# A causal attention with two feed-forward layers on one core: token blocks of 512 and 256 at 256-byte addresses, GpSimd subtractions in shorter passes, and eight PSUM banks in turn

## The chip, the core and the metric

The kernel runs on one core of a Trainium2 chip. Its engines have queues of their own and meet only at semaphores: TensorE (PE in the rows, its weight loads PEld), VectorE (DVE), ScalarE (ACT), GpSimd (POOL) and SyncE (SP), which here only issues DMA transfers. The metric is the time of one execution on the device in microseconds (us).

## The reference

```python
def _attn_ref(q, k, v, f):                       # 4 batches, 8 heads, 576 tokens, head size 64
    scores = (1.0 / np.sqrt(D)) * np.matmul(q, k.transpose(0, 1, 3, 2))
    cum = np.cumsum(np.log(np.clip(f, 0.0001, 1.0)), axis=-1)
    decay = cum[:, :, :, None] - cum[:, :, None, :]
    scores = np.where(causal, -1000000000.0, scores + decay)   # causal: above the diagonal
    attn = np.exp(scores - np.max(scores, axis=-1, keepdims=True))
    attn = attn / (np.sum(attn, axis=-1, keepdims=True) + 1e-09)
    return np.matmul(attn, v)
def _moe_ref(x, w_in, w_out):                    # x: 2304 x 512, d_ff 2048
    h = x @ w_in
    return (h * (1.0 / (1.0 + np.exp(-h)))) @ w_out
def _moe2_ref(x, w_a, w_b, w_out):               # d_ff 1536
    return ((x @ w_a) * (x @ w_b)) @ w_out
```

The attention's output, all heads side by side, is the x of the first layer, and its output the x of the second.

## The kernel before

Numbers that need more than one TensorE pass are held as a high part (rounded to the float32r format) and a low part (the rest). A product of two such numbers is three matmuls: high by high, low by high, high by low (`mm3`, lines 310 to 312; `mms`, lines 754 to 756).

**Attention.** 16 pairs of heads pass one after the other. For each pair, `load_parts` fetches q and k (`qk`, 1216 columns), makes the high part `qkh` (line 508, on ScalarE or VectorE) and the low part `qkl` (line 509, one GpSimd subtraction of all 1216 columns). `score` multiplies them into PSUM tiles `s` in groups of query blocks: 64x512, 64x384, 64x256 and 64x128 columns for the two heads of a pair side by side, and 128x288 for the last, shared block. Each is four steps: the decay in bf16, and three products of the parts. VectorE takes the masked maxima (line 584), ScalarE the exponentials (line 592). `transpose` (tiles `t_x`, `t_y`) and `attend` (tile `pv`) follow; VectorE multiplies by the inverse sums into `xf` (line 687), ScalarE makes the high part of x (line 690), GpSimd the low part (line 692, 576 columns at once).

**First chunk and decoding.** The weights come as 64-bit words and are decoded into high and low parts, 256 columns at a time: a transfer (`d`, lines 268 and 705), ScalarE (272, 707), VectorE (273 to 278, 709 to 716), ScalarE's cast (279, 718), GpSimd (280 and 281, 719 and 720). Chunk 0 of the feed-forward weights (two f-tiles of 128) is decoded and used inside the attention: `first_chunk` works on blocks of 288 tokens, four `ps` groups of three matmuls for each of two f-tiles, then g by ScalarE (766), VectorE (768), the cast `ghi` (770) and `glo` (772), then `po`, two groups for each of four output tiles. The first four of the eight blocks have a PSUM bank of their own; the last four take banks from a cycle (`BANKS`): the tag `s` has four banks, `t` two, `pv` and `mm` one each. The chunks after it are decoded into tiles `d0` to `d3`, two of each, once the attention's tiles are given up (`plan_late`).

**Order.** Up to the end of the first chunk a planner (`Plan`) sets the order on each engine from priorities and estimated times, and `keep_warm` puts idle matmuls into its first gaps. Each engine works through its row in order: an instruction that waits holds up all behind it.

**Feed-forward.** `model_kernel` then loops over chunks 1 to 12 and, in each, over the token blocks of `BLOCKS`: for each f-tile of a chunk `ff_in` (12 matmuls per product, tile `ps`, the moving operand is `x[:, part, kc, t0:t0+n]`), then `ff_out` of the block before (tile `po`, the moving operand is `ghi` or `glo`). That is 760 groups of three in `ps` and 520 in `po`, 3840 matmuls in all, 768 for each of the five blocks.

**Addresses.** `warm` is one float (4 bytes of a partition), and the tile allocator rounds up to 32 bytes. In the built program all that is allocated behind it (`x`, `acc`, the weights from chunk 1 on, `ghi`, `glo`, `g`) begins 32 bytes past a multiple of 64; `x` and the weights 32 bytes past a multiple of 256. Blocks of 464 tokens begin at 0, 1856, 3712, 5568 and 7424 bytes of a row of x, that is at 0, 64, 128, 192 and 0 bytes past a multiple of 256, counted from x's own start.

Of the kernel before, what the change touches and what calls it, by code (L numbers as in the profile page):

```python
# [9 lines left out]
F32 = mybir.dt.float32  # L10
# [3 lines left out]
AF = mybir.ActivationFunctionType  # L14
# [13 lines left out]
Q2, QK = 512 + S, 512 + S + P  # L28
# [3 lines left out]
PARTS = ((0, 128), (128, 448))  # L32
# [7 lines left out]


TAIL = NT // 2
BLOCKS = [(t, min(464, NT - t)) for t in range(0, NT, 464)]

# [159 lines left out]
def t_dve(n, fast=False):  # L206
    return 65 + n / (1.92 if fast else 0.96)
# [6 lines left out]
def t_pool(n):  # L214
    return 133 + 2.135 * n
# [14 lines left out]
def model_kernel(ctx: ExitStack, tc: tile.TileContext, qk, q0, v, f, w, out):  # L230
    nc = tc.nc
    chunks, _ = chunk_layout()

    const = ctx.enter_context(tc.tile_pool(name="const", bufs=1))
# [9 lines left out]
    dec = dram.tile([NH, 6, 2, S], BF16, name="dec")  # L244

    invs = dram.tile([NH // 2, 9, P], F32, name="invs")
    warm = const.tile([NH, 1], F32, name="warm")
    temp = ExitStack()
    dp = temp.enter_context(tc.tile_pool(name="dp", bufs=1))
    ft, one, cum = (dp.tile([NH, S], F32, name=n) for n in ("ft", "one", "cum"))  # L250
# [65 lines left out]
    gp = [None, 0, 0]  # L316
# [61 lines left out]
    NB = 288  # L378
# [12 lines left out]
    plan = Plan()  # L391
# [12 lines left out]
    def prepare():  # L404

        pr = -9
# [15 lines left out]
        plan.add("DVE", 369, lambda: nc.vector.tensor_scalar(ft, ft, 1e-4, 1.0, ALU.max, ALU.min), (), ["f"], pr)  # L422
        plan.add("ACT", 1900, lambda: nc.scalar.activation(ft, ft, AF.Ln), (), ["f"], pr)

        plan.add("ACT", 1400, lambda: nc.scalar.activation(warm, one[:, 0:1], AF.Exp), ["one", "f"], ["warm"], pr)
        plan.add("DVE", 669, lambda: nc.vector.tensor_tensor_scan(cum, one, ft, 0.0, ALU.mult, ALU.add), ["f", "one"], ["cum"], pr)
        plan.add("POOL", 133, lambda: nc.gpsimd.tensor_copy(warm, cum[:, 0:1]), ["cum"], ["warm", "go"], pr)
        plan.add("DVE", 400, lambda: nc.vector.memset(maskw, 0.0), ["cum"], [("const", 3)], -7)
        plan.add("DVE", 250, lambda: nc.vector.memset(mask2, 0.0), ["cum"], [("const", 3)], -7)
        plan.add("POOL", 250, lambda: nc.gpsimd.tensor_copy(maskw[:, -P:], maskb), [("const", 0), "cum"], [("const", 3)], -7)  # L430
# [64 lines left out]
    def load_parts(pair, pr):  # L495

        raw = buf(sb, "qkr", [P, QK], F32, f"qk_{pair}")
        hi, lo = (buf(sb, n, [P, QK], F32R, f"{n}_{pair}") for n in ("qkh", "qkl"))
        n = len(tags["dt"].bufs) % SLOTS["dt"]
        dt = Buf(tags["dt"], lambda: decays[n])  # L500
        heads[2 * pair] = heads[2 * pair + 1] = dict(s1=hi, raw=raw, hi=hi, lo=lo, dt=dt)
        plan.dma(480, 4 * P * QK, lambda: nc.sync.dma_start(raw(), qk[pair]), ["go" if pair == 1 else "dec"], [raw], pr)
        for p in range(2):
            plan.dma(400, 0, lambda p=p: nc.sync.dma_start(
                dt()[p * D:p * D + 6, :2 * S], dec[2 * pair + p].rearrange("r i t -> r (i t)")), ["dec", ("decay", n)], [(dt, p)], pr)
            plan.dma(400, 0, lambda p=p: nc.sync.dma_start(
                dt()[p * D:p * D + 6, 2 * S + p * D:2 * S + (p + 1) * D], dec[2 * pair + p, :, 0, 512:]), ["dec", ("decay", n)], [(dt, 2 + p)], pr)
        plan.add("ACT", t_act(QK, 93), lambda: nc.scalar.copy(hi(), raw()), [raw], [(hi, "h")], pr, also=[("DVE", t_dve(QK, True), lambda: nc.vector.tensor_copy(hi(), raw()))])
        (e1, d1, f1), two = ((e, d, lambda eng=eng: eng.tensor_sub(lo(), raw(), hi().bitcast(F32)))
                             for e, d, eng in (("POOL", t_pool(QK), nc.gpsimd), ("DVE", t_dve(QK) + 100, nc.vector)))  # L510
        plan.add(e1, d1, f1, [(hi, "h"), raw], [(lo, "l")], pr)

    def score(pair, group):

# [8 lines left out]
        for ib in group:  # L523
# [16 lines left out]
            for p, part, step in todo:  # L540
# [21 lines left out]
                if whole:  # L562
                    keys += [(t["s1"], "dec", 0), (t["s1"], "dec", 1), (t["s1"], "h")]
                else:
                    keys += [(t["dt"], n) for n in range(4)] + [(t["hi"], "h"), (t["lo"], "l")]
            keys = list(dict.fromkeys(keys))
            dur = 2 * (nj / 0.6 + 20) if whole else 8 * t_mm(nj) if shared else 4 * t_mm(nj)
            plan.add("PE", dur, lambda mms=mms: [mm() for mm in mms], keys, banks, pr + PRIO["s"],
# [74 lines left out]
    def attend(pair):  # L643
# [42 lines left out]
        for ps, (h0, hn) in zip(out, PARTS[::-1]):  # L686
# [2 lines left out]
                [ps] + [(rb, p, i) for p in range(2) for i in range(2)], [(xf, h0)], pr + PRIO["fin"])  # L689
        plan.add("ACT", t_act(S, 93), lambda: nc.scalar.copy(xp(0), xf()),  # L690
                 [(xf, h0) for h0, _ in PARTS], [("x", 0, b, kc)], pr + PRIO["fin"])
        plan.add("POOL", t_pool(S), lambda: nc.gpsimd.tensor_sub(xp(1), xf(), xp(0).bitcast(F32)),
                 [(xf, h0) for h0, _ in PARTS] + [("x", 0, b, kc)], [("x", 1, b, kc)], pr + PRIO["fin"])

    W0, W1, PER = 256, 256, 3

# [45 lines left out]
    def wkeys(col):  # L742
        return [("w0", col // W0), ("w0", col // W0, 1)]

    def first_chunk(b, t0, bank, sub):
# [12 lines left out]
        for t in range(nf):  # L758
            ps = bank(f"ps_{t}_{tok}")
            g = buf(gA, "g", [P, NB], F32, f"g_{t}_{tok}")  # L760
            for kc in range(KC):
                plan.add("PE", 3 * t_mm(NB), lambda ps=ps, t=t, kc=kc: mms(
                    ps, w_first(0, 0, t, kc), lambda: (big["x"][:, 0, kc, tok:tok + NB], big["x"][:, 1, kc, tok:tok + NB]),
                    kc == 0, kc == KC - 1),
                    [("x", i, b, kc) for i in range(2)] + wkeys(kc * nf * P + t * P), [ps], pr)
            plan.add("ACT", t_act(NB), lambda ps=ps, g=g: nc.scalar.activation(g(), ps()[:, :NB], AF.Tanh, scale=0.5),
                     [ps], [g], pr)
            plan.add("DVE", t_dve(NB), lambda ps=ps, g=g: nc.vector.scalar_tensor_tensor(
# [30 lines left out]
    fill_decays()  # L799

    FILL = 4
    BANKS = ('s', 't')
    fill = [(b, t0) for b in range(B) for t0 in range(0, S, NB)]
    GROUPS = (4,), (3,), (2,), (1, 0)
    for pair in range(NH // 2):
# [40 lines left out]


    mmpool[0] = ctx.enter_context(tc.tile_pool(name="mmB", bufs=8, space=PSUM))
    gp[:] = ctx.enter_context(tc.tile_pool(name="gB", bufs=2)), 3, 464
    prev = []  # L850
    for c in range(1, len(chunks)):
        pend = []
# [57 lines left out]
```

## Time and profile before

| | |
|---|---|
| median of 3 runs | 1052.15 us (1051.17 to 1052.24) |
| profiled execution, own time | 1050.7 us |
| its span, first to last instruction | 1049.0 us |
| mean granted TensorE clock | 0.996 |
| TensorE busy | 1034.1 us (99%), 5814 matmuls |
| VectorE, ScalarE, GpSimd busy | 650.6, 438.6, 325.9 us |

The own time is the span and 1.7 us around it. TensorE is hardly ever idle, so its time is the kernel's, but a matmul's record is longer than its turn: the records overlap. What a matmul costs in a dense stretch is the stretch divided by its matmuls.

### The profile page before, as it was taken

How to read it: one execution, taken by the hardware profiler on the slowest of the kernel's cores; microseconds unless marked ns; L12 is line 12 of the kernel's file. 1: busy time of each engine (PE TensorE's matmuls, PEld its weight loads, DVE VectorE, ACT ScalarE, POOL GpSimd, SP SyncE). 2: the span in 40 equal slices, each digit the busy share in tenths (PEclk: the TensorE clock that was granted, in tenths of full speed). 3: DMA queues.
4: the chain of work that ended last, by engine and by line, in shares of the span. 5: the costliest groups of instructions: out<-in, count | busy, mean ns of one | idle time of the engine just before them, and what ended most of it. 6: DMA issues, size and time to landing. Idle time of an engine off the chain costs nothing.

```text
span 1049.0 us, 16188 instructions
## 1 busy us (share of the span) xinstructions
PE 1034.1 (99%) x5814; PEld 900.1 (86%) x5814; DVE 650.6 (62%) x1545; ACT 438.6 (42%) x1074; POOL 325.9 (31%) x353
## 2 busy tenths in 40 slices
PE   8989999999999999999999999999999999999998
PEld 7757777888889899898898988988989888989987
DVE  8886555469887756846548965176475475473333
ACT  7888878854343323323225544332232231331110
POOL 5563433134333303304007762151141250340000
PEclk9999999999999999999999999999999999999999
DMA  5443331122121201201001212021021021010013
GB/s 164 151 137 116 118 104 56 40 75 71 52 81 33 88 11 41 81 1 51 31 1 57 65 57 65 1 72 51 1 81 41 21 71 31 21 60 1 28 46 108
DMA packets 34096, 62.35 MB, mean 59 GB/s; under 512 B 7004, under 2 KB 10220, under 8 KB 33984
## 3 DMA queue, kind: packets, MB, share of 16 engines
q1 hardware_dynamic: 33904, 60.87, 18.0%
q8 instruction: 46, 0.75, 0.3%
q10 hardware_dynamic: 112, 0.45, 0.2%
q14 instruction: 34, 0.28, 0.1%
HBM read 56.05 MB, written 5.23 MB: 58 GB/s over the span
## 4 chain that ended last, share of the span: by engine, by line
PE 94%; DVE 3%; ACT 1%; issue 1%; DMA 1%; POOL 0%; ACTq 0%; DVEq 0%; POOLq 0%
PE ps L310 15%; PE ps L311 15%; PE ps L312 15%; PE po L310 10%; PE po L311 10%; PE po L312 10%; PE s L558 4%; PE pv L678 3%; PE t_y L634 2%; PE t_x L634 2%; DVE p L584 1%; PE po L754 1%; PE ps L754 1%; PE po L755 1%; PE po L756 1%; PE ps L755 1%
## 5 line engine op out<-in xcount | busy, mean ns | idle before, releaser
L310 PE MATMUL ps<-x,whi 128*128 128x464 f32 (+1 forms) x760 | 282.8, 372 | 0.5 <-ACT acc L782 0.5
L311 PE MATMUL ps<-x,whi 128*128 128x464 f32 (+1 forms) x760 | 282.8, 372 | 0.0
L312 PE MATMUL ps<-x,wlo 128*128 128x464 f32 (+1 forms) x760 | 282.8, 372 | 0.0
L280 POOL TENSOR_TENSOR d<-d,whi 128x256 f32<-128x256 f32 x124 | 104.4, 850 | 436.4 <-ACT whi L279 436.2
L311 PE MATMUL po<-glo,whi 128*128 128x464 f32 (+1 forms) x520 | 192.5, 370 | 0.0
L312 PE MATMUL po<-ghi,wlo 128*128 128x464 f32 (+1 forms) x520 | 192.0, 369 | 0.0
L310 PE MATMUL po<-ghi,whi 128*128 128x464 f32 (+1 forms) x520 | 191.0, 371 | 0.0
L310 PEld LDWEIGHTS ps<-x,whi 128*128 128x128 f32 x760 | 142.7, 188 | 17.7 <-ACT acc L782 0.8
L312 PEld LDWEIGHTS ps<-x,wlo 128*128 128x128 f32 x760 | 142.6, 188 | 17.0
L311 PEld LDWEIGHTS ps<-x,whi 128*128 128x128 f32 x760 | 142.6, 188 | 16.8
L342 ACT CAST ghi<-g 128x464 fp32r<-128x464 f32 (+1 forms) x130 | 75.0, 577 | 155.5 <-DVE g L341 93.8
L272 ACT ACTIVATE d<-d 128x256 f32<-128x256 f32 x124 | 53.0, 434 | 141.7 <-DMA d<-in_w 130.7
L281 POOL TENSOR_TENSOR wlo<-d,d 128x256 fp32r<-128x256 f32 x124 | 99.7, 812 | 34.7 <-DVE d L278 33.5
L341 DVE TENSOR_TENSOR g<-g,ps 128x464 f32<-128x464 f32 (+1 forms) x60 | 37.8, 630 | 114.2 <-PE ps L312 114.2
L343 DVE TENSOR_TENSOR glo<-g,ghi 128x464 fp32r<-128x464 f32 (+1 forms) x130 | 89.8, 691 | 29.7 <-ACT ghi L342 29.2
L312 PEld LDWEIGHTS po<-ghi,wlo 128*128 128x128 f32 x520 | 97.7, 188 | 10.8
L310 PEld LDWEIGHTS po<-ghi,whi 128*128 128x128 f32 x520 | 97.7, 188 | 10.5
L311 PEld LDWEIGHTS po<-glo,whi 128*128 128x128 f32 x520 | 97.7, 188 | 10.2
L273 DVE TENSOR_SCALAR d<-d 128x256 uint32<-128x256 uint32 x124 | 46.0, 374 | 76.8 <-ACT d L272 75.6
L364 DVE SCALAR_TENSOR_TENSOR acc<-po,acc 128x464 f32<-128x464 f32 (+3 forms) x144 | 75.1, 549 | 27.6 <-PE po L312 27.5
L373 DVE TENSOR_TENSOR acc<-po,acc 128x464 f32<-128x464 f32 (+2 forms) x120 | 63.8, 552 | 26.0 <-PE po L312 25.3
L279 ACT CAST whi<-d 128x256 fp32r<-128x256 f32 x124 | 48.6, 403 | 65.5 <-DVE d L274 36.6
(121 smaller groups left out, 1440.0 us busy)
## 6 DMA issues: line engine op xcount, KB each, us to landing
d<-in_w SPq DMA_DIRECT2D x128, 256.0 KB
qk<-in_qk SPq DMA_DIRECT2D x15, 608.0 KB
vt<-in_v SPq DMA_DIRECT2D x16, 320.0 KB
rb<-invs SPq DMA_DIRECT2D x32, 128.0 KB
out_t<-acc SPq DMA_DIRECT2D x12, 232.0 KB
d2ghi<-in_w SPq DMA_DIRECT2D x8, 256.0 KB
out_t<-acc SPq DMA_DIRECT2D x4, 224.0 KB
whole<-in_q SPq DMA_DIRECT2D x2, 288.0 KB
```

The source lines that it names most:

```text
L272: nc.scalar.activation(m, high.bitcast(F32), AF.Copy, scale=2.0 ** -112)
L273: nc.vector.tensor_scalar(m.bitcast(U32), m.bitcast(U32), 3, None, ALU.logical_shift_left)
L279: nc.scalar.copy(hi, val)
L280: nc.gpsimd.tensor_sub(m, val, hi.bitcast(F32))
L281: nc.gpsimd.tensor_add(lo, m, e)
L310: nc.tensor.matmul(ps, wh, mh, start=start, stop=False)
L311: nc.tensor.matmul(ps, wh, ml, start=False, stop=False)
L312: nc.tensor.matmul(ps, wl, mh, start=False, stop=stop)
L342: nc.scalar.copy(ghi[:, t, :n], g)
L343: nc.vector.tensor_sub(glo[:, t, :n], g, ghi[:, t, :n].bitcast(F32))
L364: nc.vector.scalar_tensor_tensor(a, ps, 0.5, a, ALU.mult, ALU.add)
L373: nc.vector.tensor_add(a, ps, a)
```

## The change

Four edits. `BLOCKS` has four blocks of 512 tokens and one of 256 in place of four of 464 and one of 448, and the tiles `ghi`, `glo`, `g` are 512 wide. `warm` is 64 floats, 256 bytes: in the built program `x`, `acc`, the weights from chunk 1 on, `ghi`, `glo` and `g` then begin on multiples of 256 bytes, and with blocks of 512 every block of x and every f-tile of `ghi` and `glo` does too. GpSimd makes `qkl` in four passes of 304 columns and the low part of x in two of 288; the matmuls of `score` wait for all four, those of the first chunk for the half of x that they read. The last four blocks of the first chunk take the eight PSUM banks in turn, where they took one of `s` and one of `t` by turns.

```diff
-BLOCKS = [(t, min(464, NT - t)) for t in range(0, NT, 464)]
+BLOCKS = [(t, min(512, NT - t)) for t in range(0, NT, 512)]
...
-    warm = const.tile([NH, 1], F32, name="warm")
+    warm = const.tile([NH, 64], F32, name="warm")
...
-        (e1, d1, f1), two = ((e, d, lambda eng=eng: eng.tensor_sub(lo(), raw(), hi().bitcast(F32)))
-                             for e, d, eng in (("POOL", t_pool(QK), nc.gpsimd), ("DVE", t_dve(QK) + 100, nc.vector)))
-        plan.add(e1, d1, f1, [(hi, "h"), raw], [(lo, "l")], pr)
+
+        for c0 in range(0, QK, QK // 4):
+            c = slice(c0, c0 + QK // 4)
+            plan.add("POOL", t_pool(QK // 4), lambda c=c: nc.gpsimd.tensor_sub(lo()[:, c], raw()[:, c], hi().bitcast(F32)[:, c]),
+                     [(hi, "h"), raw], [(lo, "l", c0)], pr)
...
-                    keys += [(t["dt"], n) for n in range(4)] + [(t["hi"], "h"), (t["lo"], "l")]
+                    keys += [(t["dt"], n) for n in range(4)] + [(t["hi"], "h")] + [(t["lo"], "l", c0) for c0 in range(0, QK, QK // 4)]
...
-        plan.add("POOL", t_pool(S), lambda: nc.gpsimd.tensor_sub(xp(1), xf(), xp(0).bitcast(F32)),
-                 [(xf, h0) for h0, _ in PARTS] + [("x", 0, b, kc)], [("x", 1, b, kc)], pr + PRIO["fin"])
+        for t0 in range(0, S, NB):
+            c = slice(t0, t0 + NB)
+            plan.add("POOL", t_pool(NB), lambda c=c: nc.gpsimd.tensor_sub(xp(1)[:, c], xf()[:, c], xp(0).bitcast(F32)[:, c]),
+                     [(xf, h0) for h0, _ in PARTS] + [("x", 0, b, kc)], [("x", 1, b, kc, t0)], pr + PRIO["fin"])
...
-                    [("x", i, b, kc) for i in range(2)] + wkeys(kc * nf * P + t * P), [ps], pr)
+                    [("x", 0, b, kc), ("x", 1, b, kc, t0)] + wkeys(kc * nf * P + t * P), [ps], pr)
...
-    BANKS = ('s', 't')
+    BANKS = ('s', 's', 's', 's', 't', 'pv', 't', 'mm')
...
-    gp[:] = ctx.enter_context(tc.tile_pool(name="gB", bufs=2)), 3, 464
+    gp[:] = ctx.enter_context(tc.tile_pool(name="gB", bufs=2)), 3, 512
```

The planner orders the attention anew from these. Two places matter below.

**Place 1: from pair 3 to pair 4.** `xf_3` is the output of pair 3, `d1glo_6` and `d1g_6` are of the decoding of chunk 0's seventh piece, `p_4` are scores of pair 4. VectorE's row before:

```order
L584 ISA p_4_0_0_1137,nm_4_983<-s_4_1_0_1070,maskw_61 128x128
L584 ISA nm_4_983 128x1
L584 ISA p_4_1_0_1139,nm_4_983<-s_4_1_1_1072,maskw_61 128x128
L709 TENSOR_SCALAR d1glo_6_1100<-d1glo_6_1100 128x256
L711 SCALAR_TENSOR_TENSOR d1g_6_1143<-d2ghi_6_985,d1glo_6_1100 128x256
L687 TENSOR_TENSOR xf_3_1150<-pv_3_1_1109,rb_3_1081 128x448
```

The same place with the change:

```order
L586 ISA p_4_0_0_1152,nm_4_1002<-s_4_1_0_1089,maskw_61 128x128
L586 ISA nm_4_1002 128x1
L586 ISA p_4_1_0_1158,nm_4_1002<-s_4_1_1_1091,maskw_61 128x128
L586 ISA nm_4_1002 128x1
L689 TENSOR_TENSOR xf_3_1170<-pv_3_1_1131,rb_3_1111 128x448
```

The two decoding instructions no longer stand ahead of `xf_3`; they come earlier in the row. ScalarE's row there before, between the copies of pair 3's transposes (`th_3`) and pair 4's exponentials:

```order
L639 COPY th_3_1_1007<-t_3_y1_1056 128x512
L592 ACTIVATE p_4_1_3_1063,sm_4_1015<-p_4_1_3_1063,nm_4_983 128x512
L707 ACTIVATE d1glo_6_1100<-d2ghi_6_985 128x256
L639 COPY th_3_2_1045<-t_3_y2_1093 128x512
L508 CAST qkh_6_1107<-qk_6_951 128x1216
L592 ACTIVATE p_4_0_2_1097,sm_4_1015<-p_4_0_2_1097,nm_4_983 128x384
```

And with the change:

```order
L641 COPY th_3_0_976<-t_3_y0_1077 128x512
L722 CAST whi0_90<-d1g_6_1085 128x256
L641 COPY th_3_2_1026<-t_3_y2_1114 128x512
L508 CAST qkh_5_1128<-qk_5_760 128x1216
L508 CAST qkh_6_1154<-qk_6_989 128x1216
L594 ACTIVATE p_4_0_2_1119,sm_4_1032<-p_4_0_2_1119,nm_4_1002 128x384
```

The high part of pair 5 (`qkh_5`), which VectorE made, is now ScalarE's, behind the copy `th_3_2` and ahead of that of pair 6.

**Place 2: the attention's end.** Blocks of the first chunk are named by their first token; 1728 and 2016 are the last two, `g_0` and `g_1` their two f-tiles, `d1_2_0` and `d1_2_256` the first two pieces of chunk 2's weights. VectorE's row before, from the low part of block 1728's second f-tile on:

```order
L772 TENSOR_TENSOR glo_1728_3570<-g_1_1728_3578,ghi_1728_3558 128x288
L713 TENSOR_SCALAR d3_1_768_3612<-d2_1_768_3601 128x256
L716 SCALAR_TENSOR_TENSOR d3_1_768_3612<-d0_1_768_3523,d3_1_768_3612 128x256
L772 TENSOR_TENSOR glo_2016_3626<-g_0_2016_3587,ghi_2016_3620 128x288
L273 TENSOR_SCALAR d1_2_0_3726<-d1_2_0_3726 128x256
L274 SCALAR_TENSOR_TENSOR d3_2_0_3728<-d0_2_0_3725,d1_2_0_3726 128x256
L276 TENSOR_SCALAR d2_2_0_3727<-d3_2_0_3728 128x256
L278 SCALAR_TENSOR_TENSOR d2_2_0_3727<-d0_2_0_3725,d2_2_0_3727 128x256
L273 TENSOR_SCALAR d1_2_256_3739<-d1_2_256_3739 128x256
L274 SCALAR_TENSOR_TENSOR d3_2_256_3741<-d0_2_256_3738,d1_2_256_3739 128x256
L276 TENSOR_SCALAR d2_2_256_3740<-d3_2_256_3741 128x256
L768 SCALAR_TENSOR_TENSOR g_1_2016_3655<-g_1_2016_3655,ps_1_2016_3608 128x288
```

And with the change, from the last piece of chunk 1 on:

```order
L720 SCALAR_TENSOR_TENSOR d3_1_768_3646<-d0_1_768_3580,d3_1_768_3646 128x256
L772 SCALAR_TENSOR_TENSOR g_0_1728_3649<-g_0_1728_3649,ps_0_1728_3484 128x288
L273 TENSOR_SCALAR d1_2_0_3786<-d1_2_0_3786 128x256
L776 TENSOR_TENSOR glo_1728_3671<-g_0_1728_3649,ghi_1728_3663 128x288
L274 SCALAR_TENSOR_TENSOR d3_2_0_3788<-d0_2_0_3785,d1_2_0_3786 128x256
L772 SCALAR_TENSOR_TENSOR g_1_1728_3669<-g_1_1728_3669,ps_1_1728_3491 128x288
L772 SCALAR_TENSOR_TENSOR g_0_2016_3673<-g_0_2016_3673,ps_0_2016_3600 128x288
L276 TENSOR_SCALAR d2_2_0_3787<-d3_2_0_3788 128x256
L772 SCALAR_TENSOR_TENSOR g_1_2016_3676<-g_1_2016_3676,ps_1_2016_3605 128x288
L273 TENSOR_SCALAR d1_2_256_3799<-d1_2_256_3799 128x256
L278 SCALAR_TENSOR_TENSOR d2_2_0_3787<-d0_2_0_3785,d2_2_0_3787 128x256
L776 TENSOR_TENSOR glo_1728_3671<-g_1_1728_3669,ghi_1728_3663 128x288
```

Before, three of the four g came ahead of chunk 2's first piece; now chunk 1's last piece stands ahead of all four, and chunk 2's first two pieces between them. ScalarE's row shows the same, with the change:

```order
L770 ACTIVATE g_0_1728_3649<-ps_0_1728_3484 128x288
L272 ACTIVATE d1_2_0_3786<-d0_2_0_3785 128x256
L774 CAST ghi_1728_3663<-g_0_1728_3649 128x288
L770 ACTIVATE g_1_1728_3669<-ps_1_1728_3491 128x288
L770 ACTIVATE g_0_2016_3673<-ps_0_2016_3600 128x288
L770 ACTIVATE g_1_2016_3676<-ps_1_2016_3605 128x288
L272 ACTIVATE d1_2_256_3799<-d0_2_256_3798 128x256
```

The first instruction of chunk 2's first piece stands ahead of the first `ghi` of block 1728; before, it stood behind that of block 2016. On TensorE all `ps` groups of the last two blocks now come ahead of their `po` groups; between the last `pv` and the first `po` of block 1728 stand 43 groups of three matmuls. Before, the `po` groups of block 1728 began while block 2016's second f-tile was still to be multiplied.

## Rows read from the trace of the kernel before

**Rows 1.** Windows: start and end, length, then busy time (count) of each engine, PEclk the granted clock.

```profile
75.00:110.00 35.00, 34.95 (x296) 25.94 (x296) 20.73 (x84) 28.73 (x86) 14.19 (x8) 1.00 0.34 115
67.61:71.02 3.41, 3.20 (x16) 2.00 (x18) 3.29 (x12) 3.00 (x7) 2.28 (x2) 0.50 0.58 190
238.27:241.69 3.42, 3.04 (x14) 2.69 (x12) 2.41 (x6) 2.29 (x6) 1.74 (x3) 0.50 0.42 140
```

**Rows 2.** Waits of TensorE: total us, times, longest.

```profile
PE t_x L634 <- DVE xf L687: 3.2, 2, 2.7
PE po L754 <- DVE g L768: 2.0, 1, 2.0
```

**Rows 3.** Windows, TensorE alone: chunks 1 to 12 from first to last matmul.

```profile
241.81:1045.30 803.49, 803.48 (x3840) 1.00 0.14 45
```

**Rows 4.** Windows, tile ps alone: blocks from 0, 928, 1856 (in two chunks).

```profile
588.17:598.20 10.03, 10.03 (x48) 1.00 0.16 53
618.15:628.39 10.24, 10.24 (x48) 1.00 0.26 77
648.65:658.38 9.73, 9.73 (x48) 1.00 0.01 2
723.95:733.86 9.91, 9.91 (x48) 1.00 0.00 0
```

**Rows 5.** Windows, tile po alone: a block of 464.

```profile
613.14:618.15 5.01, 5.01 (x24) 1.00 0.38 108
```

**Rows 6.** Timeline of TensorE, first chunk, the first and thirteenth matmul of a dense run.

```profile
215.68 0.29 PE L754 MATMUL ps<-x,whi 128*128 128x288 f32 x1
...
217.27 0.29 PE L754 MATMUL ps<-x,whi 128*128 128x288 f32 x1
```

**Rows 7.** Timeline of TensorE: scores, the first step of a group (its four steps end at the next).

```profile
177.44 0.39 PE L558 MATMUL s<-decay 64*128 64x512 bf16 x2
178.37 0.34 PE L558 MATMUL s<-decay 64*128 64x384 bf16 x2
...
184.47 0.28 PE L558 MATMUL s<-decay 64*128 64x256 bf16 x2
184.94 0.23 PE L558 MATMUL s<-decay 64*128 64x128 bf16 x2
```

**Rows 8.** Timelines of ScalarE, GpSimd, VectorE and TensorE at place 1.

```profile
61.22 1.21 ACT L508 CAST qkh<-qk 128x1216 fp32r<-128x1216 f32 x1
61.18 5.57 POOL L509 TENSOR_TENSOR qkl<-qk,qkh 128x1216 fp32r<-128x1216 f32 x2 [2.36 <-PE t_y L634]
64.16 2.87 DVE L711 SCALAR_TENSOR_TENSOR d1g<-d2ghi,d1glo 128x256 uint32<-128x256 uint32 x1
71.02 0.42 DVE L711 SCALAR_TENSOR_TENSOR d1g<-d2ghi,d1glo 128x256 uint32<-128x256 uint32 x1
67.82 0.47 PE L634 MATMUL t_x<-ident,p_None 128*128 128x128 f32 x1 [2.73 <-DVE xf L687]
```

**Rows 9.** Timelines: GpSimd's passes by width, and pair 4's first score.

```profile
48.66 2.79 POOL L509 TENSOR_TENSOR qkl<-qk,qkh 128x1216 fp32r<-128x1216 f32 x1 [2.70 <-PE t_y L634]
51.45 0.30 PE L558 MATMUL s<-decay 128*128 128x288 bf16 x1
205.30 0.81 POOL L772 TENSOR_TENSOR glo<-g,ghi 128x288 fp32r<-128x288 f32 x1
```

**Rows 10.** Timelines of TensorE and ScalarE at place 2.

```profile
212.79 0.40 PE L754 MATMUL po<-ghi,whi 128*128 128x288 f32 x1
230.45 0.40 PE L755 MATMUL po<-glo,whi 128*128 128x288 f32 x1 [0.49 <-DVE glo L772]
231.08 0.44 ACT L272 ACTIVATE d<-d 128x256 f32<-128x256 f32 x1
236.67 0.40 PE L754 MATMUL po<-ghi,whi 128*128 128x288 f32 x1 [2.00 <-DVE g L768]
```

**Rows 11.** Timeline of VectorE: its last instruction.

```profile
1045.33 0.62 DVE L373 TENSOR_TENSOR acc<-po,acc 128x448 f32<-128x448 f32 x1 [0.60 <-PE po L312]
```

More of the change, by code (lines that the diff above doesn't have):

```diff
@@ L423, in prepare @@
         plan.add("ACT", 1900, lambda: nc.scalar.activation(ft, ft, AF.Ln), (), ["f"], pr)
-        plan.add("ACT", 1400, lambda: nc.scalar.activation(warm, one[:, 0:1], AF.Exp), ["one", "f"], ["warm"], pr)
+        plan.add("ACT", 1400, lambda: nc.scalar.activation(warm[:, 0:1], one[:, 0:1], AF.Exp), ["one", "f"], ["warm"], pr)
         plan.add("DVE", 669, lambda: nc.vector.tensor_tensor_scan(cum, one, ft, 0.0, ALU.mult, ALU.add), ["f", "one"], ["cum"], pr)
-        plan.add("POOL", 133, lambda: nc.gpsimd.tensor_copy(warm, cum[:, 0:1]), ["cum"], ["warm", "go"], pr)
+        plan.add("POOL", 133, lambda: nc.gpsimd.tensor_copy(warm[:, 0:1], cum[:, 0:1]), ["cum"], ["warm", "go"], pr)
         plan.add("DVE", 400, lambda: nc.vector.memset(maskw, 0.0), ["cum"], [("const", 3)], -7)
```

## The prediction

> **What bounds the kernel.** The time table comes first: TensorE is busy for 1034.1 of 1049.0 us. That is a mean over stages, so the windows come next. In the attention between two weight-decoding stretches TensorE is busy 34.95 of 35.00 us at full granted clock [rows 1], and in chunks 1 to 12 803.48 of 803.49 us for 3840 matmuls, at 1.00 too [rows 3]. There is no gap to close in either; only a shorter spacing of matmuls can gain there. The waits of TensorE show where it does stand still: 3.2 us for `xf` and 2.0 us for a g [rows 2]. Each is followed by a stretch at a granted clock of 0.50, which is the 1.2 GHz level: 3.41 us at place 1 and 3.42 us at place 2 [rows 1]. So there are three things to cost: the spacing in 803 us of feed-forward, and two waits with the slow stretch behind each.
>
> **Feed-forward: same matmuls, other sizes.** The change keeps 3840 matmuls and the same columns (5 blocks x 768 matmuls; 4 x 464 + 448 = 4 x 512 + 256 = 2304). At 2.4 GHz and one column a cycle the columns alone take 768 x 2304 / 2.4 = 737.3 us. The stretch takes 803.49 us [rows 3], so 66.2 us, 17.24 ns for each matmul, is something else. If that something were the same for every matmul, the change would be worth nothing. But it isn't: in a dense window of `ps` the block from token 0 takes 10.03 us for 48 matmuls, 209.0 ns each, and the block from 928, with the same count, engine, tile and columns, 10.24 us, 213.3 ns [rows 4]. The block of 448 takes 202.7 ns in one chunk and 206.4 in another [rows 4]. `po` has 208.8 ns at 464 [rows 5]. What differs between the first two is where the moving operand begins: 0 and 128 bytes past a multiple of 256, counted from x's start. So the extra is 209.0 - 193.3 = 15.7 ns at the favourable start and 20.0 ns at the other. After the change all blocks of x begin at the favourable offset from x's start, and x itself, which stood 32 bytes past, on a multiple of 256.
>
> For 512 columns I take the extra of block 0: 213.3 + 15.7 = 229.0 ns. For 256 the nearest row is the run of 288 columns in the first chunk, 12 matmuls in 217.27 - 215.68 = 1.59 us, 132.5 ns each, an extra of 12.5 [rows 6]: 106.7 + 12.5 = 119.2 ns. The sum is 768 x (4 x 229.0 + 119.2) = 795.0 us, or **-8.5 us**. Bounds: with 12.5 ns for all sizes but 117.5 ns for 256 (the score group of 256 columns takes 184.94 - 184.47 = 0.47 us for four steps [rows 7]) it is 768 x (4 x 225.8 + 117.5) = 783.9, -19.6 us. With 20.0 ns for all it is 768 x (4 x 233.3 + 126.7) = 814.0, +10.5 us. The one row of this trace with 512 columns is a score group, 178.37 - 177.44 = 0.93 us for four steps, 232.5 ns [rows 7]; its extra of 19.2 ns speaks for the unfavourable side, but its operands have 64 rows and lie 32 bytes past 64, so I stay with block 0, the same code line as what is forecast.
>
> By the Trainium skill, "SBUF — State Buffer", section "Who interferes with whom", TensorE waits for no one at its ports; addresses would then not matter. The two spacings of [rows 4] disagree with the rule, and the sum goes by them.
>
> The other engines of the feed-forward have as many instructions as before, wider by a tenth in four blocks and narrower in one. TensorE's 803.48 busy us cover them [rows 3]. The place to look is behind the short block: what its 48 matmuls cover is 48 x 119.2 = 5.7 us instead of 9.7. The chain from a `ps` to its low part lies under the next block's `ps` and the `po` between, so about 24 x 229.0 + 5.7 = 11 us remain for it, and I cost it at nothing.
>
> **Place 1.** Before, TensorE waits 2.73 us until 67.82 for `xf_3` [rows 8], because the VectorE instruction ahead of it (line 711) took 2.87 us instead of the 0.42 us of its next run; it runs beside GpSimd's two 1216-column passes, 5.57 us from 61.18 on, and ends 0.3 us after them [rows 8]. In the changed order that instruction is not ahead of `xf_3`. What is late next: ScalarE now casts `qkh_5` where before it went straight to `qkh_6`, at about 61.2, so until about 62.4 (1.21 us [rows 8]). GpSimd's low part then takes four passes. One of 288 columns takes 0.81 us and one of 1216 2.79 [rows 9], so four of 304 are about 4 x 0.81 x 304 / 288 = 3.4 us, and end near 65.8, where TensorE may still stand about 1.5 us before the scores of pair 5. I take 2.7 - 1.5 = 1.2 us saved, and keep the slow stretch. The four passes cost 3.4 - 2.8 = 0.6 us where a score waits for nothing else: pair 4's begins at 51.45, when the pass that began at 48.66 ends [rows 9]. Together **-0.6 us**. Bounds: if wait and slow stretch both go, 2.7 + 3.41 / 2 = 4.4 us less the same 0.6, -3.8; if nothing is saved and two pairs pay 0.6 and one VectorE instruction is blocked by a pass, 0.8, +2.0. The low part of x in two passes of 0.81 us [rows 9] is ready half at a time, and later matmuls take the second half: nothing.
>
> By the Trainium skill, the same page and section, a VectorE instruction with two SBUF inputs contends with a GpSimd instruction that reads SBUF, and the loser blocks for the whole of the other. The 2.87 us beside 0.42 agree [rows 8]; by that rule passes of 0.8 us would cap such a block at 0.8 us.
>
> **Place 2.** After the last `pv`, at 212.79 [rows 10], TensorE now has 43 groups of three matmuls of 132.5 ns, 17.1 us, and reaches the first `po` of block 1728 at 229.9. Its `ghi` stands on ScalarE behind line 272, the first step of chunk 2's first piece, which ran at 231.08 for 0.44 us [rows 10] because its transfer had then come; the cast would end near 231.9. So a wait of 2.0 us stands where 0.49 at 230.45 stood, and the later wait of 2.00 at 236.67 [rows 10] shrinks to an estimated 0.5 us, since all `ps` are finished by then. I leave the slow stretch, 3.42 us at half clock, in place, and take **0.0**. Bounds: all gone, 0.5 + 2.0 + 3.42 / 2 = 4.2, so -4.2; a second wait of 2 us, +2.0.
>
> **The end.** The last addition, 0.62 us for 448 columns [rows 11], is of 256: an estimated 0.42, as line 711 shows for that width [rows 8]. The transfer of the block behind it is of 128 KB and no longer 224. I take **-0.4 us** (bounds -0.2 and -1.3).
>
> The sum is -8.5 - 0.6 + 0.0 - 0.4 = -9.5 us. Against the profiled execution's own time, 1050.7, that is 1041.2; the median of the runs shown is 1.45 us above it, so 1042.6 us.
>
> **Rivals.** *The extra is per matmul or per column, not per address.* The feed-forward stays at 803 us and only the small terms count: 1050.7 - 1.0 + 1.45 = 1051.1 us. For it: four blocks of 464 differ by only 2% [rows 4]. Against it: they do differ. By the Trainium skill, "TensorE: Matmul & The Clock Gate", section "Back-to-back issue gap", a matmul takes N / 2.4 + 2.5 ns; count and columns stay, so by that rule the time stays as well. The trace's 209.0 ns at 464 is 13 ns above that rule.
>
> *Aligned starts take most of the extra away.* The extra becomes that of the score group of 256, 10.8 ns [rows 7]: 768 x (4 x 224.1 + 117.5) = 778.7, -24.8, less the 1.0 of the small terms, so 1026.4 us. For it: the narrow groups show that little is possible. Against it: narrow ones only.
>
> *Slower: aligned starts fall on the unfavourable setting.* High and low part of x, the weights and `ghi` then all begin on the same residue of 256, and if equal residues collide, every matmul has 20.0 ns: +10.5 - 1.0, 1061.1 us; with 20.0 for 512 alone, 768 x (4 x 233.3 + 119.2) = 808.2, +4.7 - 1.0, 1055.3 us. For it: the 512-column score group at 19.2 ns. Against it: block 0 has equal residues too, and is the faster. It decides from an average extra of 17.24 + (2.1 + 1.0) / 3.84 = 18.05 ns on (1 ns is 3.84 us).
>
> *The attention pays.* Both upper bounds, +2.0 and +2.0, with the feed-forward's gain: 1050.7 - 8.5 + 4.0 - 0.4 + 1.45 = 1047.3 us.
>
> **How the numbers follow.** Chances: the forecast 0.46, no effect of addresses 0.16, most of the extra gone 0.13, slower 0.16, the attention pays 0.09. A change of 0.2%, 2.1 us, is about what can be told from none here. Faster: the first, third and fifth, 0.68, and 0.05 of the second, where the small terms add up, 0.73. The same: 0.11 of the second and 0.01 of the fourth, 0.12. Slower: the rest of the fourth, 0.15. The range, 1027 to 1056 us, leaves out about half of the third case and the fourth where all blocks have 20.0 ns, some 0.15 in all. The forecast's own is 1038 to 1048.
>
> **What would show it.** Right: in the windows of `ps`, blocks of 512 at 11.0 us for 48 matmuls, all four alike, that of 256 at 5.7; chunks 1 to 12 in 795 us. Wrong: 11.2 us and more for 512 (slower), or 10.75 (most of the extra gone), or a step between blocks, which would mean that the start of x's row is not what counts. For place 1: line 711 no longer above 0.9 us, and no wait of 2.7 us for `xf`; if a wait of that size stands before another instruction, the step failed. For place 2: a wait for `ghi` of block 1728 near 230, and whether a stretch at clock 0.50 follows. My prediction is wrong as a whole if the feed-forward's spacing follows something that moved with the addresses in a way that block 0 doesn't show.

## The result: 1040.8 us, 1% faster

The changed kernel takes 1040.82 us (median of 4 runs, 1040.58 to 1041.57), beside 1052.16 us for the kernel before in the same comparison: a ratio of 0.9897, with a 95% interval of 0.9885 to 0.9909. The forecast was 1042.6 us. The profiled execution has an own time of 1041.05 us and a span of 1039.3 us, 9.7 us below the span of before.

The page's busy line is shown first. Then come windows of TensorE alone (start and end, length, busy time and count, granted clock, DMA share, GB/s) of chunks 1 to 12, and windows of tile `ps` alone for a block of 512 tokens and the block of 256, with busy time and count of TensorE, its weight loads, VectorE and ScalarE:

```profile
PE 1021.0 (98%) x5813; PEld 846.8 (81%) x5813; DVE 658.8 (63%) x1540; ACT 445.8 (43%) x1079; POOL 334.2 (32%) x414
```

```profile
243.95:1036.05 792.10, 790.16 (x3840) 1.00 0.14 46
```

```profile
1005.48:1016.36 10.88, 10.88 (x48) 8.82 (x47) 0.69 (x1) 1.18 (x2) 1.00 0.13 50
1021.80:1027.56 5.76, 5.76 (x48) 5.70 (x47) 0.42 (x1) 0.75 (x2) 1.00 0.26 91
```

The 3840 matmuls of the feed-forward take 792.1 us where they took 803.5 [rows 3]. A matmul of 512 columns takes 10.88 / 48 = 226.7 ns and one of 256 takes 120.0; nearly all blocks of these widths repeat those numbers. The extra beyond columns / 2.4 GHz is 13.3 ns for both, where the blocks of before had 15.7 to 20 [rows 4]. TensorE's busy time is 1.9 us short of the stretch: there are waits now, and there were none [rows 3].

Five points that both timelines of TensorE show split the 9.7 us (us):

| from | to | before | after | difference |
|---|---|---|---|---|
| start | first matmul of a score | 9.38 | 10.33 | +0.95 |
| there | first `po` after the last `pv` | 203.41 | 204.67 | +1.26 |
| there | first matmul of chunk 1 | 29.02 | 28.94 | -0.08 |
| there | end of the last matmul | 803.48 | 792.11 | -11.37 |
| there | end of the span | 3.69 | 3.23 | -0.46 |

The first score before and after, and the first `po` behind the last `pv` after (before: [rows 10]):

```profile
9.38 3.10 PE L552 MATMUL s<-whole 66*64 66x288 f32 x12
10.33 3.10 PE L554 MATMUL s<-whole 66*64 66x288 f32 x12
215.00 0.40 PE L758 MATMUL po<-ghi,whi 128*128 128x288 f32 x1
```

The first line of the table belongs to no edit: over the 14 kernels of this study the first score matmul lies between 9.18 and 10.79 us, also where nothing ahead of it was changed. So a single profile's span says nothing below 1 us, and the lines between the points say more.

Place 1, in order: TensorE's waits from 30 to 100 us (the three largest), two of them in the timeline, GpSimd's passes, the decoding instruction that was blocked (line 711 before, 715 now), and ScalarE's decoding step (line 707 before) and two casts.

```profile
PE t_y L636 <- ACT th L641: 1.6, 3, 1.0
PE s L560 <- POOL qkl L512: 0.8, 2, 0.4
PE s L560 <- DVE nm L586: 0.7, 2, 0.3
```

```profile
60.12 1.37 PE L636 MATMUL t_y<-ident,p 128*128 128x128 f32 x8 [1.03 <-ACT th L641]
68.16 0.40 PE L560 MATMUL s<-qkh,qkl 128*128 128x288 f32 x1 [0.39 <-POOL qkl L512]
...
56.14 1.63 POOL L696 TENSOR_TENSOR x<-xf,x 128x288 fp32r<-128x288 f32 x2 [1.80 <-ACT x L692]
64.89 4.01 POOL L512 TENSOR_TENSOR qkl<-qk,qkh 128x304 fp32r<-128x304 f32 x5
...
57.13 0.92 DVE L715 SCALAR_TENSOR_TENSOR d1g<-d2ghi,d1glo 128x256 uint32<-128x256 uint32 x1
...
61.31 0.42 DVE L715 SCALAR_TENSOR_TENSOR d1g<-d2ghi,d1glo 128x256 uint32<-128x256 uint32 x1
...
59.48 0.44 ACT L711 ACTIVATE d1glo<-d2ghi 128x256 f32<-128x256 f32 x1 [0.96 <-POOL wlo L724]
63.60 2.32 ACT L508 CAST qkh<-qk 128x1216 fp32r<-128x1216 f32 x2
```

The wait of 2.7 us for `xf` [rows 2] is down to 0.2. The decoding instruction takes 0.92 us beside passes of 288 columns that end at 57.77, and 0.42 alone, where it took 2.87 [rows 8]. It is blocked more often, though: of its eight executions in the attention, six now take 0.82 to 1.05 us, where two took 1.47 and 2.87, and each of them ends 0.3 us after the end of a GpSimd pass. The largest wait, 1.03 us, is new: ScalarE's copies `th` stand behind a decoding step that waited 0.96 us for GpSimd.

The slow stretch is gone too: windows of 34 to 75 us and 75 to 110 us show a granted clock of 1.00, but in the second TensorE is now idle for 1.2 us, where it was idle for 0.05 [rows 1]. From the first score to the first `po` after the last `pv` all of TensorE's idle time is 5.97 us, beside 5.15 before: many short waits took the place of the long one.

```profile
34.00:75.00 41.00, 37.50 (x319) 26.22 (x318) 35.79 (x112) 36.30 (x101) 28.50 (x36) 1.00 0.42 135
75.00:110.00 35.00, 33.76 (x292) 24.70 (x289) 19.66 (x79) 28.33 (x83) 15.90 (x20) 1.00 0.37 117
```

Place 2, timeline of TensorE (rows with a wait, in brackets; first the one ahead of chunk 1 in the kernel before), then of ScalarE ahead of chunk 1:

```profile
241.81 0.48 PE L310 MATMUL ps<-x,whi 128*128 128x464 f32 x1 [0.50 <-ACT acc L782]
...
233.11 0.40 PE L758 MATMUL po<-ghi,whi 128*128 128x288 f32 x1 [0.62 <-ACT ghi L774]
234.02 0.40 PE L759 MATMUL po<-glo,whi 128*128 128x288 f32 x1 [0.51 <-DVE glo L776]
235.97 0.40 PE L758 MATMUL po<-ghi,whi 128*128 128x288 f32 x1 [0.22 <-ACT ghi L774]
237.09 0.40 PE L759 MATMUL po<-glo,whi 128*128 128x288 f32 x1 [0.73 <-DVE glo L776]
243.95 0.50 PE L310 MATMUL ps<-x,whi 128*128 128x512 f32 x1 [1.95 <-ACT acc L786]
```

```profile
242.56 0.43 ACT L272 ACTIVATE d<-d 128x256 f32<-128x256 f32 x1 [0.77 <-DMA d<-in_w]
242.89 1.00 ACT L786 ACTIVATE acc<-po 128x288 f32<-128x288 f32 x3
```

Waits of 0.49 and 2.00 us [rows 10], and one of 0.50 ahead of chunk 1, have become four of 0.2 to 0.7 and one of 1.95 ahead of chunk 1: the last three evacuations of the first chunk stand on ScalarE behind line 272, which waited for its transfer until 242.56. The slow stretch of before [rows 1] is gone; the window from 225 to 242 us shows 1.00. Waits and clock nearly cancel.

```profile
225.00:242.00 17.00, 14.91 (x105) 13.79 (x103) 14.20 (x30) 10.52 (x29) 9.28 (x13) 1.00 0.28 88
```

That the slow stretch is gone here can't be put down to the edits. Of the 14 kernels of this study eight have it (a granted clock of 0.90 to 0.91 from 225 us to chunk 1) and wait 0.50 us ahead of chunk 1; six, some of them with the attention of before, have 1.00 and wait 1.3 to 2.1 us. Either way chunk 1 begins 28.4 to 29.3 us after the first `po` behind the last `pv`, right after the end of the last evacuation.

In the feed-forward the timeline of TensorE has three more waits: one at the first `po` of chunk 1, and two at the end of the first layer, in the `po` of block 1536, behind the short block's `ps`. The last row is VectorE's last addition, 0.42 us where it took 0.62 [rows 11].

```profile
250.41 0.96 PE L310 MATMUL po<-ghi,whi 128*128 128x512 f32 x3 [0.73 <-ACT ghi L342]
...
583.45 0.50 PE L310 MATMUL po<-ghi,whi 128*128 128x512 f32 x1 [0.60 <-ACT ghi L342]
584.56 0.50 PE L311 MATMUL po<-glo,whi 128*128 128x512 f32 x1 [0.60 <-DVE glo L343]
...
1036.09 0.42 DVE L373 TENSOR_TENSOR acc<-po,acc 128x256 f32<-128x256 f32 x1 [0.29 <-PE po L312]
```

### The profile page after: what moved, and what is told of

Read it like the earlier page. It is cut to its first block, busy times and chain, and to the rows that moved or that the text cites. A ratio compares the mean times of both kernels' runs of the same rounds, so it can differ in the third digit from the quotient of the medians.

```text
span 1039.3 us, 16203 instructions
## 1 busy us (share of the span) xinstructions
PE 1021.0 (98%) x5813; PEld 846.8 (81%) x5813; DVE 658.8 (63%) x1540; ACT 445.8 (43%) x1079; POOL 334.2 (32%) x414
## 4 chain that ended last, share of the span: by engine, by line
PE 86%; DVE 3%; ACT 1%; DMA 1%; issue 1%; POOL 0%; ACTq 0%; SPq 0%; POOLq 0%; DVEq 0%
PE ps L311 14%; PE ps L310 14%; PE ps L312 14%; PE po L311 10%; PE po L310 10%; PE po L312 10%; PE s L560 4%; PE pv L680 3%; PE t_x L636 2%; PE t_y L636 2%; DMA d<-in_w 1%; PE ps L758 1%; PE po L758 1%; PE ps L760 1%; PE ps L759 1%; DVE d L274 1%
## 5 line engine op out<-in xcount | busy, mean ns | idle before, releaser
L310 PE MATMUL ps<-x,whi 128*128 128x512 f32 (+1 forms) x760 | 279.8, 368 | 1.9 <-ACT acc L786 1.9
L311 PE MATMUL ps<-x,whi 128*128 128x512 f32 (+1 forms) x760 | 279.7, 368 | 0.0
L312 PE MATMUL ps<-x,wlo 128*128 128x512 f32 (+1 forms) x760 | 279.5, 368 | 0.0
L311 PE MATMUL po<-glo,whi 128*128 128x512 f32 (+1 forms) x520 | 191.5, 368 | 0.6 <-DVE glo L343 0.6
L312 PE MATMUL po<-ghi,wlo 128*128 128x512 f32 (+1 forms) x520 | 191.3, 368 | 0.0
L310 PE MATMUL po<-ghi,whi 128*128 128x512 f32 (+1 forms) x520 | 189.8, 368 | 1.3 <-ACT ghi L342 1.3
L342 ACT CAST ghi<-g 128x512 fp32r<-128x512 f32 (+1 forms) x130 | 75.1, 578 | 148.8 <-DVE g L341 95.3
L341 DVE TENSOR_TENSOR g<-g,ps 128x512 f32<-128x512 f32 (+1 forms) x60 | 37.9, 631 | 116.3 <-PE ps L312 115.8
L343 DVE TENSOR_TENSOR glo<-g,ghi 128x512 fp32r<-128x512 f32 (+1 forms) x130 | 89.0, 685 | 34.2 <-ACT ghi L342 33.5
L364 DVE SCALAR_TENSOR_TENSOR acc<-po,acc 128x512 f32<-128x512 f32 (+3 forms) x144 | 75.8, 552 | 22.8 <-PE po L312 22.3
L373 DVE TENSOR_TENSOR acc<-po,acc 128x512 f32<-128x512 f32 (+2 forms) x120 | 64.6, 554 | 25.5 <-PE po L312 25.0
```

Source lines behind the costliest of these rows:

```text
L310: nc.tensor.matmul(ps, wh, mh, start=start, stop=False)
L311: nc.tensor.matmul(ps, wh, ml, start=False, stop=False)
L312: nc.tensor.matmul(ps, wl, mh, start=False, stop=stop)
L342: nc.scalar.copy(ghi[:, t, :n], g)
L343: nc.vector.tensor_sub(glo[:, t, :n], g, ghi[:, t, :n].bitcast(F32))
L364: nc.vector.scalar_tensor_tensor(a, ps, 0.5, a, ALU.mult, ALU.add)
```

## Experiments

Each kernel is timed against the kernel before in its own comparison, so ratios are what compares; "chunk 1" is the start of chunk 1, "stretch" that of chunks 1 to 12.

**The blocks alone.**

```diff
-BLOCKS = [(t, min(464, NT - t)) for t in range(0, NT, 464)]
+BLOCKS = [(t, min(512, NT - t)) for t in range(0, NT, 512)]
-    ... name="gB", bufs=2)), 3, 464
+    ... name="gB", bufs=2)), 3, 512
```

> Only the blocks change (512 and 256); everything in the feed-forward begins 32 bytes past a multiple of 256, the attention is that of before. Theory A (the extra beyond columns / 2.4 depends on where the rows begin): 512 columns keep the extra of the block from token 0 before, 15.7 ns, so 229.0 ns a matmul, 256 columns 119 to 122; chunks 1 to 12 take 795 to 797 us and the median is about 1044 us. Rival B (the sizes alone do it, whole multiples of 256 bytes whatever the start): 226.7 and 119.8 ns as in the changed kernel, 791 us with its stalls, 1039.5 us.

1039.72 us, 0.9888 (0.9873 to 0.9903); stretch 792.26 us. Windows of `ps`, a block of 512 that begins 32 bytes past a multiple of 256:

```profile
1004.49:1015.37 10.88, 10.88 (x48) 8.82 (x47) 0.69 (x1) 1.18 (x2) 1.00 0.13 50
```

It is the 10.88 us of the changed kernel. Theory A, on which the forecast stood, falls: the start address of the whole tile does not give the 226.7 ns.

**The start addresses alone.**

```diff
-    warm = const.tile([NH, 1], F32, name="warm")
+    warm = const.tile([NH, 64], F32, name="warm")
...
```

> Only the 256-byte float tile changes: x and the weights begin on a multiple of 256, the blocks of 464 on 0, 64, 128, 192 and (448) 64 less or more of it; attention as before. Theory A: the block from token 0 falls from 209.0 to 206.5 ns (193.3 + 13.2), the other blocks change too, by up to some ns; chunks 1 to 12 take 790 to 800 us, the median is 1039 to 1049. Rival B (the sizes do it): the spacings stay, 803.5 us, median 1052.

1051.47 us, 0.9999 (0.9990 to 1.0009); stretch 803.48 us, as before [rows 3] to a hundredth. Windows of `ps`, the blocks from 0 and 928, for which [rows 4] have 10.03 and 10.24:

```profile
587.99:598.02 10.03, 10.03 (x48) 8.83 (x47) 1.21 (x2) 0.54 (x1) 1.00 0.17 53
617.98:628.22 10.24, 10.24 (x48) 8.79 (x47) 0.00 (x0) 0.54 (x1) 1.00 0.25 77
```

The spacings stay at 209.0 and 213.3 ns: the 256-byte alignment of the base is worth nothing. (Other shifts of the base than these 32 bytes were not tried.)

**The feed-forward's edits together**: both diffs above, the attention of before.

> Blocks and start addresses together, attention as before. Theories A and B both: 226.7 and 119.8 ns, chunks 1 to 12 in 791 to 792 us (788.4 by these spacings and 2 to 3 us of stalls behind the short block). Theory C (the attention's edits cost 2.1 us at the start of chunk 1): chunk 1 begins at 241.8 and no longer at 243.9, median about 1039 us. Rival D (those 2.1 us come from the moved addresses or differ from run to run): chunk 1 begins near 243.9 here too, 1041.

1038.73 us, 0.9880 (0.9865 to 0.9895); stretch 791.93 us, chunk 1 at 242.33. The attention's edits are not needed for the gain.

**The attention's edits alone**: the changed kernel with the blocks, tiles and `warm` of before.

> GpSimd's shorter passes and the eight banks alone; blocks of 464 and all start addresses of the feed-forward as before. Theory C: chunk 1 begins near 243.9, the feed-forward takes 803.5 us as before, median about 1054 us. Rival D: chunk 1 begins near 241.8, median about 1052. By both the 2.7 us wait for xf of pair 3 and the half-clock stretch behind it are gone.

1052.45 us, 1.0012 (1.0002 to 1.0021); chunk 1 at 244.01, stretch 803.52. Theory C holds for the start of chunk 1, but 1.0 us of that start is the variable beginning, and the median lies nearer rival D's 1052. From the first score to the first `po` after the last `pv` it is 204.51 us, as in the changed kernel, beside 203.4 to 204.1 in the ten kernels that have the old passes. So these edits lose about 0.9 us there.

**Where the blocks begin inside x.** Start addresses of 256 bytes, the attention of before, other blocks; three kernels, one execution each.

```diff
+BLOCKS = [(0, 464), (464, 512), (976, 512), (1488, 512), (2000, 304)]     (shifted)
+BLOCKS = [(0, 448), (448, 448), (896, 448), (1344, 448), (1792, 512)]     (448s)
+BLOCKS = [(0, 480), (480, 480), (960, 480), (1440, 480), (1920, 384)]     (480s)
```

> Blocks of 464, 512, 512, 512 and 304, start address and attention as in the run with the feed-forward's edits alone; three blocks of 512 now begin 64 bytes past a multiple of 256 and none on a multiple of 2048. Theory B (the size of a block sets its spacing): the 512-column blocks stay at 226.7 ns and the first block has 209 ns as before. Theory A2 (what counts is where a block's rows begin, by 64 bytes, which moving everything by 32 bytes left as it was): the 512-column blocks go up by 3 ns or more.

> Blocks of 448 four times and 512, the rest as in the run with the feed-forward's edits alone; all blocks begin on multiples of 256 bytes. Theory A2: 448 columns get the 13.3 ns of the aligned blocks, 200.0 ns. Theory B: 448 columns keep 202.7 to 206.4 ns, since the size is at fault, and 512 has 226.7; chunks 1 to 12 then take 768 x (4 x 205 + 226.7) = 804 us.

> Blocks of 480 four times and 384, the rest as in the run with the feed-forward's edits alone; every second block of 480 begins 128 bytes past a multiple of 256. Theory B in the form that a matmul takes its columns, rounded up to a multiple of 32, and 32 more cycles: 480 takes 213.3 ns and 384 takes 173.3, all blocks alike, chunks 1 to 12 in 788.5 us. Theory B in the form that only multiples of 256 columns go well: 480 takes 217 ns and more. Theory A2: the first and third block of 480 differ from the second and fourth.

They took 1044.82, 1045.07 and 1049.35 us, with stretches of 796.2, 797.4 and 801.6 us. Windows of `ps`: a block of 512 that begins 64 bytes past a multiple of 256; a block of 448; and the second, fourth and first block of 480.

```profile
974.96:985.96 11.00, 11.00 (x48) 8.82 (x48) 0.69 (x1) 1.17 (x2) 1.00 0.01 1
```

```profile
1003.57:1013.30 9.73, 9.73 (x48) 8.83 (x47) 0.62 (x1) 1.07 (x2) 1.00 0.13 49
```

```profile
979.34:989.90 10.56, 10.56 (x48) 8.79 (x48) 0.66 (x1) 1.12 (x2) 1.00 0.01 2
1010.71:1020.95 10.24, 10.24 (x48) 8.79 (x47) 0.65 (x1) 1.12 (x2) 1.00 0.13 50
964.77:975.17 10.40, 10.40 (x48) 8.81 (x47) 0.65 (x1) 1.12 (x2) 1.00 0.00 0
```

Both the width and the start inside x matter, and something else too. At 512 columns a start 64 bytes off costs 229.2 - 226.7 = 2.5 ns. At 448 columns the extra is 16.0 ns, though all starts are multiples of 256 bytes: the width is at fault. At 480 three starts give 213.3, 216.7 and 220.0 ns, extras of 13.3 to 20.0; the second and the fourth block both begin 128 bytes past a multiple of 256 and differ by 6.7 ns, so the start counted by 256 bytes does not decide. Neither theory holds alone, nor does rounding up to 32 columns, by which 480 would always take 213.3.

The something else is in [rows 4]: the block from 1856, of one width and one start, took 9.73 us in one chunk and 9.91 in the other. In the kernel before it takes the lower spacing in five of chunks 1 to 12 and the higher in seven, by turns in the second layer. With four blocks of 448 every one takes the lower, and chunks 1 to 12 take 797.4 us and not the 804 of theory B. What differs between the chunks in the program is the tile of the weights (two take turns), and the PSUM bank and the buffers of `ghi` and `glo` that a block gets; no run separates them.

**A longer last block.** Blocks of 512 three times and 384 twice, the rest as with the feed-forward's edits.

> Blocks of 512 three times and 384 twice, the rest as in the run with the feed-forward's edits alone. Theory E (the short block of 256 covers too little, which stalls TensorE for about 2.5 us at the end of the first layer): with 384 columns the cover is half as long again, the stalls of 0.8 and 0.9 us are gone, and with 173.3 ns for 384 columns chunks 1 to 12 take 788.5 to 790 us, the median about 1036.5 us. Rival (the stall comes from the end of the first layer whatever the block): 791 to 792 us, 1038.7.

1039.99 us, 0.9890 (0.9874 to 0.9907); stretch 792.07 us, no better. One of the two stalls of the first layer's end is gone, the other stays:

```profile
581.56 0.44 PE L311 MATMUL po<-glo,whi 128*128 128x384 f32 x1 [0.73 <-DVE glo L343]
```

So the cover was part of the cause. What was saved is lost behind changes of width, of which there are six in a chunk here and four with the feed-forward's edits: over chunks 1 to 12 the first eight matmuls behind each change take 2.2 us more than their steady spacings, beside 0.7 us there (up to 185 ns at 384 columns, where 173 is steady).

**The short block first.** (0, 256), then four of 512, the rest as with the feed-forward's edits.

> Feed-forward's edits with the block of 256 first instead of last; attention as before. Theory E2 (the stalls of 0.8 and 0.9 us at the end of the first layer come from the short block's cover there): with it first they are gone or stand elsewhere for less; chunks 1 to 12 in 789 to 791 us, median 1036.5 to 1038. Rival (they come from the last chunk's casts, whatever block is there): 791.9 us, 1038.7.

1039.24 us, 0.9887 (0.9870 to 0.9904); stretch 791.83 us. The stalls move and change their cause, and are no shorter (two waits of 1.7 us together, beside two of 1.3 in the kernel with the feed-forward's edits alone):

```profile
589.53 0.50 PE L310 MATMUL po<-ghi,whi 128*128 128x512 f32 x1 [0.40 <-DVE acc L364]
593.87 0.50 PE L310 MATMUL po<-ghi,whi 128*128 128x512 f32 x1 [1.28 <-DVE acc L364]
```

ScalarE or VectorE is late at the end of the first layer wherever the short block stands. Both theories on these stalls were too simple.

**The attention's edits apart**, each on top of the feed-forward's edits: the eight banks alone; all of GpSimd's passes with the two banks; and the four passes of `qkl` alone, the low part of x in one.

> Feed-forward's edits and the eight banks, GpSimd's passes as before. Theory F (of the attention's edits it is the shorter passes that cost, about 1.2 us up to the last pv, and the banks cost or give under 0.5 us): the wait of 2.7 us for xf of pair 3 is back, chunk 1 begins at 241.8 to 242.8, median 1038 to 1039.5. Rival G (the banks cost it): chunk 1 begins at 243.5 or later, median 1040.5.

> The changed kernel with the two banks of before: feed-forward's edits and all of GpSimd's shorter passes. Theory F: no 2.7 us wait, but many short ones between 75 and 140 us, chunk 1 begins at 243.3 to 244.5, median 1040 to 1041. Rival G: chunk 1 begins at 242 to 242.8, median 1038.7.

> Feed-forward's edits and the four passes of qkl alone; the low part of x in one pass, two banks. Theory F1 (the four passes of qkl cost, by their 0.6 us more on the path of scores): as the run with all passes, 1040 to 1041. Theory F2 (the halves of x's low part cost, by GpSimd's time before the first chunk): as the feed-forward's edits alone, chunk 1 at 242.3 or, with the wait of place 1 gone, 240, median 1036.5 to 1038.7.

| | median | ratio | first score to first `po` after the last `pv` | from there to chunk 1 |
|---|---|---|---|---|
| feed-forward's edits | 1038.73 | 0.9880 (0.9865 to 0.9895) | 203.84 | 28.45 |
| and eight banks | 1039.67 | 0.9891 (0.9876 to 0.9905) | 204.08 | 29.04 |
| and all passes | 1040.69 | 0.9899 (0.9884 to 0.9914) | 204.68 | 29.27 |
| and passes of `qkl` | 1037.67 | 0.9871 (0.9856 to 0.9885) | 202.55 | 28.84 |
| the changed kernel | 1040.82 | 0.9897 (0.9885 to 0.9909) | 204.67 | 28.94 |

The banks do nothing that can be told: 28.4 to 29.3 us to chunk 1 with two, 28.9 to 29.1 with eight. The passes split. Those of `qkl` alone take 0.8 to 1.5 us off the attention (203.4 to 204.1 in the ten kernels with the old passes), and with the halves of x's low part it is 2.1 us longer again (204.68 less 202.55). Windows of 75 to 110 us, all passes and then those of `qkl` alone, TensorE only:

```profile
75.00:110.00 35.00, 33.70 (x285) 1.00 0.37 111
```

```profile
75.00:110.00 35.00, 34.55 (x293) 1.00 0.34 111
```

With `qkl` alone TensorE is busy for 0.85 us longer in there; the rest isn't in one place. TensorE's waits from 30 to 100 us in that kernel, the two largest:

```profile
PE t_x L636 <- DVE xf L689: 2.0, 3, 1.2
PE s L560 <- DVE nm L586: 0.9, 2, 0.6
```

The wait for `xf` is 1.2 us where it was 2.7, and no wait for `qkl` is left. Theory F1 falls, and the times are those of F2. The two kernels differ in the order that the planner makes as well as in the passes; which of the two costs the 2.1 us was not separated. The traces point at the order: in neither does TensorE wait for a low part of x, and with the halves ScalarE makes five of the casts `qkh` and not three, and from 30 to 100 us TensorE waits 1.6 us and not 0.4 for its copies `th`. This kernel is the fastest that was run, 3.1 us under the changed one, though the intervals of the two ratios still touch; all its four executions (1037.0 to 1038.5 us) are below all four of the kernel with all passes (1040.1 to 1041.2), which was timed beside it.

## Why the prediction was right

**Feed-forward: right in sign, by a reason that fell in part.** The forecast was -8.5 us, measured -11.37. The step that failed is "for 512 columns I take the extra of block 0", because that block began favourably. The extra of 15.7 ns did not carry over to 512 columns, nor was it the address that changed: with x moved to a multiple of 256 bytes a block of 464 keeps its spacing, and a block of 512 has 13.3 ns at either base. For 256 columns the 12.5 ns taken from the run of 288 measured 13.1 to 13.3. By spacing alone the sum is 768 x (4 x 226.7 + 119.8) = 788.4 us, -15.1. The bounds held it. The first rival, the same extra per matmul or per column, falls too: same count, same columns, and 11 us less. Its doubt about the addresses was right: moved alone, they give nothing. By that rule of the Trainium skill ("TensorE: Matmul & The Clock Gate", "Back-to-back issue gap"), which the page gives for a single matmul by itself, a matmul of 512 takes an estimated 215.8 ns; the trace's 226.7 are 10.9 more, and the measured spacing is what decides.

**Behind the short block: a cost where the forecast had none.** Of the 15.1 us, 3.7 are given back. Most is at three waits, two of them behind the short block: 1.9 us of idle time, and about 1 us more by the starts of the matmuls around them. About 0.5 us is in the first matmuls after a change of width, which take up to 236 ns and not 227. The forecast counted 48 matmuls of 256 columns as cover. That is the second layer's number; at the end of the first layer there are 24, 2.9 us, with ScalarE and VectorE also busy making the next x and decoding weights.

**Place 1: -0.6 forecast, +1.26 measured.** The cause of the old wait was right, and what the edits take away was put too low: wait and slow stretch both go, 4.4 us by the forecast's own bound, and before the scores of pair 5 0.39 us are left where 1.5 were forecast. The four passes cost two waits of 0.4. A blocked instruction takes up to 1.05 us, over the 0.9 that the forecast named; the 0.63 us above its 0.42 alone stay under a pass of 0.8, and so the cap by the length of a pass, which the Trainium skill gives ("SBUF — State Buffer", "Who interferes with whom"), agrees. With the passes of `qkl` alone the same stretch is 0.9 us shorter than before. What failed is "the low part of x in two passes: nothing": that edit, with the order that the planner makes from it, costs 2.1 us.

**Place 2: 0.0 forecast, -0.08 measured**, with other contents: 2.1 us of waits for ghi and glo, in four pieces where the forecast had 2.0 in one, then 1.95 us for an evacuation, where I had a later wait of 0.5 and the slow stretch, which is gone. That the sum is right is luck.

**The end: -0.4 forecast, -0.46 measured.**

**The total.** From profile to profile the change is -9.7 us where -9.5 was forecast. That is luck in part: the feed-forward gave 2.9 us more, place 1 took 1.9 more, and 0.95 us is the variable beginning.

**The rivals.** "Slower" was decided by an extra of 18.05 ns; it is 13.3 steady. (Its two times, 1061.1 and 1055.3, are 0.5 us lower than their own terms add up to.) "Aligned starts take most of the extra away" asked for 10.8 ns and didn't come. "The attention pays" came in part, +1.26 of the +4 it asked for.

## What to carry to other kernels

Where a long stretch is bound by one engine, read the spacing of its instructions by width before anything else: here 13.3 ns or 20 ns beyond the columns decided 11 us, and a block size is changed in one line. What a neighbouring width costs can't be read from the one in use; time two or three. Where a planner makes the order, time each split of a pass by itself: of two here one gained about 1 us and the other, with the order that came of it, lost 2, though in neither kernel TensorE waited for the part that was split.

## What the runs showed of the hardware

The spacing of float32r matmuls of 128x128 weights depends on the width and on where the moving rows begin inside their tile, but not on these two alone: extras beyond columns / 2.4 of 13.3 ns at 256, 384 and 512 columns (starts at multiples of 256 bytes), 11.2 at 304, 16.0 at 448 (19.8 in seven of the twelve chunks of the kernel before, at one and the same start), 15.7 to 20.0 at 464, and 13.3, 16.7 or 20.0 at 480 by the block. A start 64 bytes off costs 2.5 ns at 512; moving everything by 32 bytes costs nothing. What in the chip makes these steps stays open: no run here separates it.

VectorE's decoding instruction (line 711, now 715), which reads two tiles, ended 0.3 us after the GpSimd subtraction that was under way when it began, each time: it took 2.87 us beside passes of 1216 columns, 1.47 beside one of 576, 0.82 to 1.05 beside passes of 288 and 304, and 0.42 alone.
